# Moving GpSimd's share of the first half of a fused attention and MLP kernel to VectorE, with a scheduler that counts overlapping operations

## The chip, the cores and the metric

The kernel runs on one core of a Trainium2 chip. The metric is the device time of one execution in microseconds (us). Five engines work side by side: PE (TensorE, the matmuls), DVE (VectorE), ACT (ScalarE), POOL (GpSimd) and SP (SyncE, which issues nearly all DMAs). Each executes its own list of instructions strictly in order, and semaphores make one list wait for another.

## The reference, cut to what matters

Attention within chunks of 64 rows, and then an MLP with a hard-swish gate, all in 32-bit floating point:

```python
scores = scale * np.matmul(q_c, k_c.transpose(0, 1, 2, 4, 3))   # chunks of 64 rows, head size 64
scores = scores - np.max(scores, axis=-1, keepdims=True)
attn = np.exp(scores)
attn = attn / (np.sum(attn, axis=-1, keepdims=True) + 1e-09)
out = np.matmul(attn, v_c)            # 8 batches, 8 heads, 576 rows: x is 4608 x 512
h = x @ w_in                          # 512 x 2048
g = h * np.clip(h + 3.0, 0.0, 6.0) / 6.0
return (g @ w_out).astype(np.float32) # 2048 x 512
```

## The kernel before, in words

The 4608 tokens are cut into nine blocks of 512. Block 0 goes through the MLP in the plain way; blocks 1 to 8 go as four pairs (s = 0 to 3), and each pair's two matrix products are done by a scheme with seven block products in place of eight (Winograd's form of Strassen's), which needs sums and differences of the operands. Each product is made in three passes of PE over a high and a low part of both operands (lines 351 to 353), so every operand is split: ACT casts the high part, and another engine subtracts it from the whole, which leaves the low part.

All work is a list of named steps, each with an engine, a cost, the steps it comes after, and what it issues (`work.add`). `Schedule.order` plays the list through once at build time: an engine whose time is free takes, of the steps that are ready, the one that is due first. The order in which steps are taken is the order of the instructions on each engine. The costs are used for nothing else. One rule in it charges a DVE step whose name begins with an entry of `BOTH` extra time while a POOL step is planned beside it (`SHARED`).

The steps that matter here, by their names (u is 0 to 15, p is 0 to 7, k is 0 to 7):

- `lowera{k}`, `lowerb{k}` (L210): the low part of a piece of w_in (a) or w_out (b). `LOWER_ON_POOL` puts b2 to b7 on POOL. Each w_in piece is needed by two tiles `a{j}`, `b{j}` of the first product on PE, each w_out piece by two tiles `c{j}` of the second.
- `whole{u}`, `comb{u}`, `top{u}`, `less{u}s`, `send{u}` (L450, L455, L460, L463, L468): the sums of the weights for the pairs: whole weights (from SBUF on DVE, from DRAM on SP), four subtractions of 128x256, the high part on ACT, the low part, and the store to DRAM on SP. u = 0 to 7 is w_out, 8 to 15 w_in. `LESS_ON_POOL` puts `less0s` to `less7s` on POOL, `COMBS` puts `comb8` to `comb11` there. The tile that `comb` works in, and the one that `top` and `less` write, have two buffers each: `whole{u}` waits for `less{u-2}s`, and `top{u}` for `send{u-2}`.
- `x0.s0` to `x0.s3b` (L570, L574): sums of the first pair's inputs; all but `x0.s0`, `x0.s0c` and `x0.s1` stand on POOL. `x0.5l`, `x0.6l`, `x0.7l`, `x0.4l` (L581) are their low parts.
- `t1.0.p`, `t2.0.p` (L962, L965): sums of the first pair's gates, on POOL. The same sums of the later pairs (L947, L949) are on POOL too, and stay there.
- `gate...` (L377, L761), `u2`, `u4`, `s7`, `s3`, `s4` (L873): DVE's work on each tile that PE finishes. PE's accumulators are few (2 of one kind, 4 of the other), so a late gate stops PE.
- `max`, `sum`, `share` and `turn` with a unit's number: softmax of half a block and its transposes on PE; `turn30` waits for `share30` (L281).
- `f{i}.0.p`: the seven first products of pair 0 (i is the product, p the tile, here 4 to 7). `f5.0.4` is the first that reads sums of weights: `top12`, `less12s`, and `x0.5l`.
- `s0.n`: the second products of pair 0; `ul0.i.k` and `m0.i.k` (L984, L987, L990) make their operands on DVE.

On PE the program runs in this order: softmax of block 0, then the tiles of block 0 and of half of blocks 1 and 2 (to about 172 us), the first products of pair 0 (to 226 us), its second products (to about 313 us), and then pairs 1 to 3, which differ only in where the next pair's attention stands.

Of the kernel before, what the change touches and what calls it, by code (L numbers as in the profile page):

```python
# [31 lines left out]
NFP = NFT // 2  # L32
NPL = 4
# [8 lines left out]
FILL = (2.0, 4.0)  # L42
LAG = 2
ROWS = ["30", "31", "40", "41"]
XDVE = ["x0.s0c"]
SHARED = 0.6
BOTH = ("lower", "join", "whole", "less", "comb", "share", "glow", "ul", "m0", "m1", "m2", "m3", "x0.", "x1.", "x2.", "x3.")
LESS_ON_POOL = list(range(8))
XPOOL = []
ULPOOL = []  # L50
LOWER_ON_POOL = [f"b{i}" for i in range(2, 8)]
APART = 2
EDGE = 32
HASTE = 5.0
# [4 lines left out]
PART = STEP / 4  # L59
SECOND = STEP * (17 + 2 * NPL) + PART * 7 * (NFP - NPL)  # L60
STEPS = SECOND - PART * 7 * (NFP - NPL)
COMBS = [8, 9, 10, 11]


class Schedule:
# [21 lines left out]
    def order(self):  # L87
        then = {n: [] for n in self.steps}
        left = {}
        for n, (_, _, after, _) in self.steps.items():  # L90
            left[n] = len(after)
            for a in after:
                then[a].append(n)
        sorted_, more = [n for n in self.steps if not left[n]], dict(left)
        for n in sorted_:
            for m in then[n]:
                more[m] -= 1
                if not more[m]:
                    sorted_.append(m)
        assert len(sorted_) == len(self.steps)  # L100
        latest = {}
        for n in reversed(sorted_):
            latest[n] = min([self.due[n]] + [latest[m] - self.steps[m][1] - SETTLE for m in then[n]])
        queue = {n: (latest[n] if self.first[n] is None else self.first[n] - 1e6, i) for i, n in enumerate(self.steps)}
        ready = [(0.0, i, n) for i, n in enumerate(self.steps) if not left[n]]
        heapq.heapify(ready)
        waiting, free, at, now = {}, {}, {}, 0.0
        while len(at) < len(self.steps):
            while ready and ready[0][0] <= now:
                _, _, n = heapq.heappop(ready)  # L110
                heapq.heappush(waiting.setdefault(self.steps[n][0], []), (queue[n], n))
            for engine, names in waiting.items():
                if names and free.get(engine, 0.0) <= now:
                    (due, _), n = names[0]
                    end = now + self.steps[n][1]
                    if engine == "DVE" and n.startswith(BOTH):
                        end += SHARED * max(0.0, min(end, free.get("POOL", 0.0)) - now)
                    soon = [t for t, _, m in ready if self.steps[m][0] == engine and 2 * t < now + end and queue[m][0] < due - HASTE]
                    if soon and engine != "SP":
                        free[engine] = min(soon)  # L120
                        continue
                    heapq.heappop(names)
                    at[n], free[engine] = (now, end), end
                    for m in then[n]:
                        left[m] -= 1
                        if not left[m]:
                            t = max(at[a][1] + (0.0 if a[:5] == m[:5] == "fetch" else LAND if self.steps[a][0] == "SP" else 0.0 if self.steps[a][0] == self.steps[m][0] == "PE" else SETTLE)
                                    for a in self.steps[m][2])
                            heapq.heappush(ready, (t, len(at), m))
            now = min([t for t, *_ in ready] + [max(now, free[e]) for e, names in waiting.items() if names], default=now)  # L130
        return sorted(at.items(), key=lambda s: s[1][0])
# [3 lines left out]
def tile_kernel(ctx: ExitStack, tc: tile.TileContext, qk_in, v_in, weights, out):  # L135
# [293 lines left out]
    def in_dram(m, p):  # L429

        return "ab"[m] + str(p // 2) in KEPT
# [405 lines left out]
    for u in [*range(NFP), *range(NFP + NPL, 2 * NFP), *range(NFP, NFP + NPL)]:  # L837
        m, p = 1 - u // NFP, u % NFP
        whole, combine, high, lower, send, send_own = sum_steps(m, p)
        due = STEPS - 8 + 4 * (u - 7) if u < NFP else STEPS - 3 + PART * 7 * (p - NPL) if p >= NPL else SECOND + 10 + 12 * p  # L840
        last = [f"f3.0.{p}"] if u >= NFP + NPL else []
        work.add(f"own{u}", "SP", 2.35, ["lower" + "ab"[m] + str((p + NFP * f) // 2) for f in range(2)], send_own)
        work.add(f"whole{u}", *(("SP", 1.57) if in_dram(m, p) else ("DVE", 1.38)), ["room", *work.take("a", 2, f"whole{u}", [f"less{u}s"])], whole)
        work.add(f"comb{u}", *(("POOL", 4.2, [f"whole{u}"], lambda f=combine: f(POOL)) if u in COMBS else ("DVE", 1.70, [f"whole{u}"], lambda f=combine: f(DVE))))
        work.add(f"top{u}", "ACT", 1.05, [f"comb{u}", *work.take("hl", 2, f"top{u}", [f"send{u}", *last])], high)
        work.add(f"less{u}s", *(("POOL", 2.5, [f"top{u}"], lambda f=lower: f(POOL)) if u in LESS_ON_POOL else ("DVE", 1.22, [f"top{u}"], lambda f=lower: f(DVE))), due=due)
        work.add(f"send{u}", "SP", 3.15, [f"less{u}s"], send, due=due + (4 if u < NFP else 12))
        stored += [f"own{u}", f"send{u}"]
# [104 lines left out]
    def add_units(s):  # L953
        plain = {"gate2.": NFT, "gate4.": NFT + NFP, "gate7.": 2 * NFT + NFP}

        def both(name, pp):
            return [f"gate{plain[name] + 2 * pp + k}" if s == 0 and 2 * pp < NPL and name in plain else f"{name}{s}.{2 * pp + k}" for k in range(2)]

        if s == 0:
            for p in range(NFP):  # L960
                gates = [f"gate{2 * NFT + p}", f"gate{NFT + p}"] if p < NPL else [f"gate3.0.{p}", f"gate2.0.{p}"]
                work.add(f"t1.0.{p}", "POOL", 1.45, gates, lambda p=p: POOL.tensor_tensor(  # L962
                    out=gate_of(0, 1, p), in0=gate_of(0, 1, p), in1=gate_of(0, 0, p), op=ALU.subtract))
                free = {0: [f"out{et}" for et in range(NET)], 1: [f"u2.0.{NFP - 1}"], 2: [f"s7.0.{NFP - 1}"], 3: [f"s3.0.{NFP - 1}", f"s4.0.{NFP - 1}"]}[p // 2]
                work.add(f"t2.0.{p}", "POOL", 1.45, [f"t1.0.{p}", f"gate{2 * NFT + NFP + p}" if p < NPL else f"gate7.0.{p}", *free], lambda p=p: POOL.tensor_tensor(  # L965
                    out=t2_of(p), in0=gate_of(1, 1, p), in1=gate_of(0, 1, p), op=ALU.subtract))
        made_by = {1: "gate2.", 5: "t1.", 6: "t2.", 2: "gate4.", 3: "gate7."}
        for i in ORDER_B:
            for pp in range(NFP // 2):
                high, low = f"uh{s}.{i}.{pp}", f"ul{s}.{i}.{pp}"  # L970
                r, c = WHERE[i]
                src = lambda i=i, pp=pp, r=r, c=c: t2s_of(pp) if i == 6 else gates_of(r, c, pp)
                after = both(made_by[i], pp) if i in made_by else [f"m{s}.{i}.{pp}"]

                slot, before = next_slot(s, high, [f"s{s}.{NFP * ORDER_B.index(i) + 2 * pp + 1}"
                                                   if not (s == NSUP - 1 and i == 3) else f"s{s}.{SLOTS - 4 + pp}"])

                def top(i=i, pp=pp, src=src, slot=slot):
                    g_ops[s, i, pp] = w_tile(f"a{slot}", F32R)
                    ACT.copy(out=g_ops[s, i, pp][:, :, 0], in_=src())  # L980

                work.add(high, "ACT", 1.05, [*after, *before], top)
                on = (s, i, pp) in ULPOOL
                work.add(low, *(("POOL", 2.5) if on else ("DVE", 1.22)), [high], lambda i=i, pp=pp, src=src, on=POOL if on else DVE: on.tensor_tensor(  # L984
                    out=g_ops[s, i, pp][:, :, 1], in0=src(), in1=g_ops[s, i, pp][:, :, 0].bitcast(F32), op=ALU.subtract))
                if i == 5:
                    work.add(f"m{s}.7.{pp}", "DVE", 1.22, [f"ul{s}.1.{pp}", *both("t2.", pp)], lambda pp=pp: DVE.tensor_tensor(  # L987
                        out=gates_of(0, 0, pp), in0=t2s_of(pp), in1=gates_of(0, 0, pp), op=ALU.subtract))
                elif i == 6:
                    work.add(f"m{s}.4.{pp}", "DVE", 1.22, [f"ul{s}.5.{pp}", *both("t2.", pp), *both("gate4.", pp)], lambda pp=pp: DVE.tensor_tensor(  # L990
                        out=gates_of(0, 1, pp), in0=gates_of(1, 0, pp), in1=t2s_of(pp), op=ALU.subtract))
# [135 lines left out]
```

## Time and profile before

| | us |
|---|---|
| median of 3 runs | 799.24 (799.12 to 799.25) |
| the profiled execution | 800.39 |
| its span, first to last instruction | 798.6 |
| PE busy in the span | 778.8 |
| DVE busy in the span | 647.6 |
| POOL busy in the span | 161.2 |

The median lies 1.15 us under the profiled execution, and 1.8 us of that execution lie outside its span. "Busy" counts the time in which an engine had an instruction in execution; an instruction that is held up counts as busy too. A timeline row gives the start, the duration, the engine, the line, the operation, the tiles with their shape and how many instructions are merged, and in brackets how long the engine was idle before it and which instruction ended that.

### The profile page before, as it was taken

To read this page: it belongs to the slowest core of one execution; us is meant where nothing else is said; L and a number is where in the kernel's file an instruction comes from. 1 tells how busy PE (TensorE), PEld (TensorE's weight loads), DVE (VectorE), ACT (ScalarE), POOL (GpSimd) and SP (SyncE) were. 2 spreads that over 40 slices of the span, in tenths; PEclk is the share of its full clock that TensorE was granted. 3 is DMA by queue.
4 is the path that set the end of the run, shared out by engine and by line. 5 is a ranking of instruction groups with operands and counts; after the bars stand their busy time and mean duration, and the time that the engine had idled before them with its cause. 6 is when DMAs were issued, how large, how long until landed. Compare 5 with 4: busy or idle time off the path is not lost.

```text
span 798.6 us, 14046 instructions
## 1 busy us (share of the span) xinstructions
PE 778.8 (98%) x5601; PEld 637.9 (80%) x5603; DVE 647.6 (81%) x758; ACT 396.8 (50%) x593; POOL 161.2 (20%) x105
## 2 busy tenths in 40 slices
PE   8999999978999999999999999999999999999998
PEld 4788878766787888888888888888888888888887
DVE  6898999999899869868898786787998657669851
ACT  3998753356477654334654443335653424355330
POOL 0011242663290120322210001332100013221000
PEclk9999999998999999999999999999999999999999
DMA  9998998864957999666665876576656665566572
GB/s 374 384 412 293 347 324 306 264 219 142 304 190 251 332 313 368 204 195 241 209 241 198 285 268 205 190 241 246 215 195 219 222 207 193 190 197 209 192 232 106
DMA packets 69425, 198.05 MB, mean 248 GB/s; under 512 B 7024, under 2 KB 19568, under 8 KB 65008
## 3 DMA queue, kind: packets, MB, share of 16 engines
q1 hardware_dynamic: 69216, 197.03, 72.0%
q8 instruction: 44, 0.72, 0.4%
q14 instruction: 21, 0.17, 0.1%
q10 hardware_dynamic: 144, 0.13, 0.0%
HBM read 153.09 MB, written 44.04 MB: 247 GB/s over the span
## 4 chain that ended last, share of the span: by engine, by line
PE 80%; DVE 14%; DMA 2%; ACT 2%; issue 1%; POOL 1%; SPq 0%; DVEq 0%; ACTq 0%; POOLq 0%
PE acc L351 18%; PE acc L352 18%; PE acc L353 18%; PE h L352 6%; PE h L351 6%; PE h L353 6%; DVE a L455 4%; PE two L243 2%; PE two L293 2%; PE h L319 2%; DVE wb L761 1%; DVE a L450 1%; DVE e L281 1%; DMA qk<-qk_in 1%; DVE wa L984 1%
## 5 line engine op out<-in xcount | busy, mean ns | idle before, releaser
L351 PE MATMUL acc<-wa,ws 128*128 128x512 f32 (+1 forms) x536 | 209.3, 391 | 0.0
L353 PE MATMUL acc<-wa,ws 128*128 128x512 f32 (+1 forms) x536 | 207.8, 388 | 0.0
L352 PE MATMUL acc<-wa,ws 128*128 128x512 f32 (+1 forms) x536 | 207.8, 388 | 0.0
L980 ACT CAST wa<-wb 128x1024 fp32r<-128x1024 f32 x96 | 100.5, 1053 | 99.4 <-PE acc L353 60.3
L984 DVE TENSOR_TENSOR wa<-wb,wa 128x1024 fp32r<-128x1024 f32 x96 | 126.1, 1322 | 26.4 <-ACT wa L980 26.3
L351 PEld LDWEIGHTS acc<-wa,ws 128*128 128x128 f32 x536 | 100.7, 188 | 20.9 <-issue 0.3
L353 PEld LDWEIGHTS acc<-wa,ws 128*128 128x128 f32 x536 | 100.6, 188 | 20.6
L352 PEld LDWEIGHTS acc<-wa,ws 128*128 128x128 f32 x536 | 100.7, 188 | 20.1
L947 POOL TENSOR_TENSOR wb<-wb 128x512 f32<-128x512 f32 x24 | 32.0, 1332 | 361.0 <-DVE wb L761 361.0
L758 ACT ACTIVATE r<-acc,half 128x512 f32<-128x512 f32 x90 | 61.5, 687 | 41.6 <-DVE acc L873 36.8
L758 ACT ACTIVATE r<-h,half 128x512 f32<-128x512 f32 x38 | 26.2, 689 | 98.6 <-DVE h L873 93.9
L761 DVE SCALAR_TENSOR_TENSOR wb<-r,acc 128x512 f32<-128x512 f32 x90 | 60.8, 681 | 5.6 <-ACT r L758 5.3
L352 PE MATMUL h<-wa,ws 128*128 128x512 f32 (+1 forms) x144 | 55.2, 383 | 0.0
L353 PE MATMUL h<-wa,ws 128*128 128x512 f32 (+1 forms) x144 | 55.2, 383 | 0.0
L351 PE MATMUL h<-wa,ws 128*128 128x512 f32 (+1 forms) x144 | 55.2, 383 | 0.0
L873 DVE TENSOR_TENSOR u<-h,p 128x512 f32<-128x512 f32 x32 | 22.0, 690 | 31.6 <-PE h L353 31.5
L873 DVE TENSOR_TENSOR acc<-acc,u 128x512 f32<-128x512 f32 x48 | 33.2, 697 | 10.3 <-PE acc L353 10.0
L455 DVE TENSOR_TENSOR a<-a 128x256 f32<-128x256 f32 x48 | 40.2, 838 | 1.2
L949 POOL TENSOR_TENSOR g<-wb,wb 128x512 f32<-128x512 f32 x24 | 38.0, 1584 | 1.9
L761 DVE SCALAR_TENSOR_TENSOR wb<-r,h 128x512 f32<-128x512 f32 x38 | 25.9, 683 | 12.6 <-ACT r L758 12.6
L210 POOL TENSOR_TENSOR wb<-u,wb 128x1024 fp32r<-128x1024 f32 x6 | 16.9, 2832 | 88.8 <-ACT wb L207 72.6
L351 PE MATMUL acc<-wa,wa 128*128 128x512 f32 x88 | 34.9, 396 | 0.0
(202 smaller groups left out, 1496.1 us busy)
## 6 DMA issues: line engine op xcount, KB each, us to landing
ws<-b SPq DMA_DIRECT2D x84, 512.0 KB, 4.6
ws<-a SPq DMA_DIRECT2D x72, 512.0 KB, 4.4
qk<-qk_in SPq DMA_DIRECT2D x17, 1024.0 KB, 7.7
wa<-b SPq DMA_DIRECT2D x28, 512.0 KB, 5.7
a<-wa SPq DMA_DIRECT2D x40, 256.0 KB, 5.8
v<-v_in SPq DMA_DIRECT2D x17, 512.0 KB, 5.2
wa<-w_in_out SPq DMA_DIRECT2D x8, 1024.0 KB, 11.2
wb<-w_in_out SPq DMA_DIRECT2D x8, 1024.0 KB, 9.5
```

What stands on the lines that cost most here:

```text
L210: engine.tensor_tensor(out=w[i][:, :, 1], in0=t["a"], in1=w[i][:, :, 0].bitcast(F32), op=ALU.subtract)
L351: PE.matmul(ps, lhsT=a_h, rhs=b_h, start=first, stop=False, skip_group_check=more)
L352: PE.matmul(ps, lhsT=a_h, rhs=b_l, start=False, stop=False, skip_group_check=more)
L353: PE.matmul(ps, lhsT=a_l, rhs=b_h, start=False, stop=last, skip_group_check=more)
L455: engine.tensor_tensor(out=to, in0=x, in1=y, op=op)
L758: ACT.activation(out=t["r"], in_=ps(), func=AF.Relu, bias=half, scale=1.0 / 6.0)
L761: work.add("gate" + name, "DVE", 0.69, ["relu" + name, *more], lambda: DVE.scalar_tensor_tensor(out=out(), in0=t["r"], scalar=1.0, in1=ps( ...
L873: return lambda: DVE.tensor_tensor(out=out(), in0=x(), in1=y(), op=ALU.add)
L947: work.add(id_("t1."), "POOL", 1.45, [id_("gate3."), id_("gate2.")], lambda f=gq: POOL.tensor_tensor(out=f(0, 1), in0=f(0, 1), in1=f(0, 0) ...
L949: work.add(id_("t2."), "POOL", 1.45, [id_("t1."), id_("gate7.")], lambda f=gq, p=p: POOL.tensor_tensor(out=t2_of(p), in0=f(1, 1), in1=f(0, ...
L980: ACT.copy(out=g_ops[s, i, pp][:, :, 0], in_=src())
L984: work.add(low, *(("POOL", 2.5) if on else ("DVE", 1.22)), [high], lambda i=i, pp=pp, src=src, on=POOL if on else DVE: on.tensor_tensor(ou ...
```

## The change

Every table that puts work of the first half on POOL is emptied, and the t1 and t2 steps of pair 0 go to DVE; POOL's first arithmetic instruction is now `t1.1.0`, of the second pair. In `Schedule.order` an engine is counted as free 0.08 us (DVE) or 0.1 us (ACT) before its step ends, and two planned costs of DVE steps are changed (`whole` 1.38 to 1.28, `comb` 1.70 to 1.88). These costs only set the order.

```diff
-XDVE = ["x0.s0c"]
+XDVE = ["x0.s0c", "x0.s2", "x0.s2b", "x0.s3", "x0.s3b"]
 SHARED = 0.6
+OVERLAP = {"DVE": 0.08, "ACT": 0.1}
...
-LESS_ON_POOL = list(range(8))
+LESS_ON_POOL = []
 XPOOL = []
+TPOOL = False
 ULPOOL = []
-LOWER_ON_POOL = [f"b{i}" for i in range(2, 8)]
+LOWER_ON_POOL = []
...
-COMBS = [8, 9, 10, 11]
+COMBS = []
...
-                    at[n], free[engine] = (now, end), end
+                    at[n], free[engine] = (now, end), end - OVERLAP.get(engine, 0.0)
...
-        work.add(f"whole{u}", *(("SP", 1.57) if in_dram(m, p) else ("DVE", 1.38)), ...
+        work.add(f"whole{u}", *(("SP", 1.57) if in_dram(m, p) else ("DVE", 1.28)), ...
-        work.add(f"comb{u}", *(("POOL", 4.2, ...) if u in COMBS else ("DVE", 1.70, ...)))
+        work.add(f"comb{u}", *(("POOL", 4.2, ...) if u in COMBS else ("DVE", 1.88, ...)))
...
-                work.add(f"t1.0.{p}", "POOL", 1.45, gates, lambda p=p: POOL.tensor_tensor(
+                work.add(f"t1.0.{p}", *(("POOL", 1.45) if TPOOL else ("DVE", 0.69)), gates, lambda p=p: (POOL if TPOOL else DVE).tensor_tensor(
...
-                work.add(f"t2.0.{p}", "POOL", 1.45, [f"t1.0.{p}", ...
+                work.add(f"t2.0.{p}", *(("POOL", 1.45) if TPOOL else ("DVE", 0.69)), [f"t1.0.{p}", ...
```

Line numbers after the change are 2 higher. Three places in the order of instructions follow; in them `hl` is the tile of `top` and `less`, `a` the tile of `comb`, `wa`, `wb` and `g` with numbers are buffers of operands and gates.

First, DVE between `comb12` and `share30`, before: `comb12`, `x0.6l`, `less12s`, `gate34`, `x0.7l`, `gate35`, `comb13`, two small steps, `u2.0.4`, `share30`.

```order
L455 TENSOR_TENSOR a<-a 128x256 x4
L581 TENSOR_TENSOR wa_1902<-wb_1406,wa_1902 128x2x512
L463 TENSOR_TENSOR hl<-a,hl 128x4x256
L761 SCALAR_TENSOR_TENSOR wb_1592<-r,h 128x512
L581 TENSOR_TENSOR wa_1949<-wb_1783,wa_1949 128x2x512
L761 SCALAR_TENSOR_TENSOR wb_1592<-r,acc 128x512
L455 TENSOR_TENSOR a<-a 128x256 x4
L277 TENSOR_SCALAR z<-z 128x16
L278 RECIPROCAL z<-z 128x16
L873 TENSOR_TENSOR g_2022<-h,g_1994 128x512
L281 TENSOR_TENSOR e<-e,z 128x1024
```

The same stretch now, from the row after the one that follows `comb12`: `x0.s3`, `gate34`, `x0.6l`, `less12s`, `x0.7l`, `gate35`, `less7s`, `x0.s3b`, two small steps, `gate42`, `share30`.

```order
L576 TENSOR_TENSOR wb_1841<-xc,wb_1412 128x1024
L763 SCALAR_TENSOR_TENSOR wb_1602<-r,h 128x512
L583 TENSOR_TENSOR wa_1908<-wb_1412,wa_1908 128x2x512
L465 TENSOR_TENSOR hl<-a,hl 128x4x256
L583 TENSOR_TENSOR wa_1940<-wb_1841,wa_1940 128x2x512
L763 SCALAR_TENSOR_TENSOR wb_1602<-r,acc 128x512
L465 TENSOR_TENSOR hl<-a,hl 128x4x256
L576 TENSOR_TENSOR wb_1841<-wb_1841,xc 128x1024
L279 TENSOR_SCALAR z<-z 128x16
L280 RECIPROCAL z<-z 128x16
L763 SCALAR_TENSOR_TENSOR wb_1739<-r,h 128x512
L283 TENSOR_TENSOR e<-e,z 128x1024
```

`x0.s3`, `less7s` and `x0.s3b` came in from POOL, `gate41` (not shown, it follows `comb12` now) and `gate42` moved, and `comb13` went behind `share30`.

Second, DVE around `share31` (L281), before: `m0.7.0`, `ul0.5.1`, `ul0.5.2`, `m0.7.1`, two small steps, `share31`, `ul0.5.3`, `ul0.6.0`, `ul0.6.1`.

```order
L987 TENSOR_TENSOR wb_1388<-g_2009,wb_1388 128x2x512
L984 TENSOR_TENSOR wa_2497<-wb_1592,wa_2497 128x2x512
L984 TENSOR_TENSOR wa_2515<-wb_2140,wa_2515 128x2x512
L987 TENSOR_TENSOR wb_1592<-g_2418,wb_1592 128x2x512
L277 TENSOR_SCALAR z<-z 128x16
L278 RECIPROCAL z<-z 128x16
L281 TENSOR_TENSOR e<-e,z 128x1024
L984 TENSOR_TENSOR wa_2546<-wb_1406,wa_2546 128x2x512
L984 TENSOR_TENSOR wa_2551<-g_2009,wa_2551 128x2x512
L984 TENSOR_TENSOR wa_2560<-g_2418,wa_2560 128x2x512
```

Now: `ul0.5.1`, two small steps, `share31`, `ul0.5.2`, `ul0.5.3`, five of the eight t2 steps, `ul0.6.0`, and two more t2 steps.

```order
L986 TENSOR_TENSOR wa_2471<-wb_1602,wa_2471 128x2x512
L279 TENSOR_SCALAR z<-z 128x16
L280 RECIPROCAL z<-z 128x16
L283 TENSOR_TENSOR e<-e,z 128x1024
L986 TENSOR_TENSOR wa_2491<-wb_2078,wa_2491 128x2x512
L986 TENSOR_TENSOR wa_2495<-wb_1412,wa_2495 128x2x512
L967 TENSOR_TENSOR g_2527<-wb_1497,wb_1362 128x512 x2
L967 TENSOR_TENSOR g_2536<-wb_1739,wb_1602 128x512 x2
L967 TENSOR_TENSOR g_2550<-wb_2065,wb_2078 128x512
L986 TENSOR_TENSOR wa_2538<-g_2527,wa_2538 128x2x512
L967 TENSOR_TENSOR g_2550<-wb_2065,wb_2078 128x512
L967 TENSOR_TENSOR g_2571<-wb_1841,wb_1412 128x512
```

Two m steps and `ul0.5.2` went behind `share31`, and the t2 steps stand between `share31` and the next softmax.

Third, PE around `turn11` (L293), before: the last three passes of tile `b11`, `turn11`, the first pass of `c7`.

```order
L351 MATMUL h<-xd,wa_847 128x512
L352 MATMUL h<-xd,wa_847 128x512
L353 MATMUL h<-xd,wa_847 128x512
L293 MATMUL two<-ident,e 128x128 x8
L351 MATMUL acc<-g_836,wb_783 128x512
```

Now: the last three passes of tile `a11`, `turn11`, the first pass of `b11`.

```order
L353 MATMUL h<-xa,wa_833 128x512
L354 MATMUL h<-xa,wa_833 128x512
L355 MATMUL h<-xa,wa_833 128x512
L295 MATMUL two<-ident,e 128x128 x8
L353 MATMUL h<-xd,wa_833 128x512
```

`turn11` stands six passes earlier. PE's order differs in seven more places by one to four steps; among them `turn31` stands ahead of `s0.11` now, six passes earlier too. PE's instructions are the same in number.

## Rows read from the trace of the kernel before

**Rows 1.** The page's busy time, share and instructions of each engine.

```profile
PE 778.8 (98%) x5601; PEld 637.9 (80%) x5603; DVE 647.6 (81%) x758; ACT 396.8 (50%) x593; POOL 161.2 (20%) x105
```

**Rows 2.** Timeline of PE: the instructions before which it was idle longest after 100 us.

```profile
105.64 0.50 PE L351 MATMUL h<-xb,wa 128*128 128x512 f32 x1 [0.28 <-DVE r L377]
...
108.29 1.06 PE L293 MATMUL two<-ident,e 128*128 128x128 f32 x8 [0.99 <-DVE e L281]
...
152.29 0.50 PE L352 MATMUL h<-xd,wa 128*128 128x512 f32 x1 [1.51 <-DVE xd L340]
...
178.77 0.80 PE L351 MATMUL acc<-wa,hl 128*128 128x512 f32 x1 [4.65 <-ACT hl L460]
...
189.63 1.06 PE L293 MATMUL two<-ident,e 128*128 128x128 f32 x8 [2.27 <-DVE e L281]
...
213.22 0.50 PE L351 MATMUL acc<-xd,hl 128*128 128x512 f32 x1 [0.64 <-DVE g L873]
...
243.09 1.06 PE L293 MATMUL two<-ident,e 128*128 128x128 f32 x8 [1.01 <-DVE e L281]
```

**Rows 3.** Windows of 5 us; last three columns: PE's granted clock, DMA share, GB/s.

```profile
180.00:185.00 5.00, 4.97 (x13) 3.94 (x14) 4.93 (x6) 5.00 (x18) 4.35 (x3) 0.56 0.81 267
...
190.00:195.00 5.00, 4.84 (x96) 3.68 (x98) 5.00 (x8) 2.29 (x3) 0.00 (x0) 1.00 0.00 0
```

**Rows 4.** Timeline of PE: passes of one shape that follow each other.

```profile
184.45 0.40 PE L351 MATMUL acc<-wa,hl 128*128 128x512 f32 x1
...
184.92 0.39 PE L353 MATMUL acc<-wa,hl 128*128 128x512 f32 x1
185.15 0.39 PE L351 MATMUL acc<-wa,hl 128*128 128x512 f32 x1
```

**Rows 5.** Groups by line and shape, DVE, 40 to 178 us: busy us, mean ns.

```profile
L455 DVE TENSOR_TENSOR a<-a 128x256 f32<-128x256 f32 x36 | 30.8, 855 | 0.9
...
L384 DVE TENSOR_TENSOR g<-r,g 128x512 fp32r<-128x512 f32 x14 | 13.1, 937 | 0.4 <-ACT g L381 0.4
L450 DVE TENSOR_TENSOR a<-wb 128x512 f32<-128x512 f32 x12 | 9.9, 863 | 0.0
...
L281 DVE TENSOR_TENSOR e<-e,z 128x1024 f32<-128x1024 f32 x4 | 8.1, 2023 | 0.0
```

**Rows 6.** Single lines over the whole span: shortest, median and longest in ns.

```profile
L384 DVE TENSOR_TENSOR g<-r,g x16: 679/684/2477, 31.3 to 120.6; 128x512 fp32r<-128x512 f32 x16
...
L281 DVE TENSOR_TENSOR e<-e,z x17: 1211/1218/3022, 14.0 to 604.8; 128x1024 f32<-128x1024 f32 x17
```

**Rows 7.** Timeline of DVE: two combs, two wholes, and three low parts in a row.

```profile
110.47 1.28 DVE L450 TENSOR_TENSOR a<-wb 128x512 f32<-128x512 f32 x2
...
149.25 1.79 DVE L455 TENSOR_TENSOR a<-a 128x256 f32<-128x256 f32 x4
...
172.09 5.51 DVE L455 TENSOR_TENSOR a<-a 128x256 f32<-128x256 f32 x4
...
244.00 3.49 DVE L984 TENSOR_TENSOR wa<-g,wa 128x1024 fp32r<-128x1024 f32 x3
```

**Rows 8.** Groups of POOL, 40 to 300 us; idle time before each and its ends.

```profile
L463 POOL TENSOR_TENSOR hl<-a,hl 128x1024 fp32r<-128x1024 f32 x8 | 20.7, 2585 | 36.5 <-ACT hl L460 23.0 <-DMA qk<-qk_in 9.5 <-DMA b<-hl 4.1
```

**Rows 9.** A window of 20 us: busy PE, PEld, DVE, ACT, POOL, clock, DMA.

```profile
60.00:80.00 20.00, 20.00 (x211) 16.36 (x210) 16.74 (x22) 17.45 (x21) 3.10 (x1) 1.00 0.85 293
```

**Rows 10.** Timelines of DVE and PE: `share11`, `turn11`, `share31`, `share40`, `turn40`.

```profile
77.73 1.22 DVE L281 TENSOR_TENSOR e<-e,z 128x1024 f32<-128x1024 f32 x1
...
79.87 0.81 PE L293 MATMUL two<-ident,e 128*128 128x128 f32 x6
...
241.72 1.23 DVE L281 TENSOR_TENSOR e<-e,z 128x1024 f32<-128x1024 f32 x1
...
263.42 1.22 DVE L281 TENSOR_TENSOR e<-e,z 128x1024 f32<-128x1024 f32 x1
...
267.38 1.03 PE L293 MATMUL two<-ident,e 128*128 128x128 f32 x8
```

More of the change, by code (lines that the diff above doesn't have):

```diff
@@ L842, in tile_kernel @@
         work.add(f"own{u}", "SP", 2.35, ["lower" + "ab"[m] + str((p + NFP * f) // 2) for f in range(2)], send_own)
-        work.add(f"whole{u}", *(("SP", 1.57) if in_dram(m, p) else ("DVE", 1.38)), ["room", *work.take("a", 2, f"whole{u}", [f"less{u}s"])], whole)
-        work.add(f"comb{u}", *(("POOL", 4.2, [f"whole{u}"], lambda f=combine: f(POOL)) if u in COMBS else ("DVE", 1.70, [f"whole{u}"], lambda f=combine: f(DVE))))
+        work.add(f"whole{u}", *(("SP", 1.57) if in_dram(m, p) else ("DVE", 1.28)), ["room", *work.take("a", 2, f"whole{u}", [f"less{u}s"])], whole)
+        work.add(f"comb{u}", *(("POOL", 4.2, [f"whole{u}"], lambda f=combine: f(POOL)) if u in COMBS else ("DVE", 1.88, [f"whole{u}"], lambda f=combine: f(DVE))))
         work.add(f"top{u}", "ACT", 1.05, [f"comb{u}", *work.take("hl", 2, f"top{u}", [f"send{u}", *last])], high)
@@ L961, in add_units @@
                 gates = [f"gate{2 * NFT + p}", f"gate{NFT + p}"] if p < NPL else [f"gate3.0.{p}", f"gate2.0.{p}"]
-                work.add(f"t1.0.{p}", "POOL", 1.45, gates, lambda p=p: POOL.tensor_tensor(
+                work.add(f"t1.0.{p}", *(("POOL", 1.45) if TPOOL else ("DVE", 0.69)), gates, lambda p=p: (POOL if TPOOL else DVE).tensor_tensor(
                     out=gate_of(0, 1, p), in0=gate_of(0, 1, p), in1=gate_of(0, 0, p), op=ALU.subtract))
                 free = {0: [f"out{et}" for et in range(NET)], 1: [f"u2.0.{NFP - 1}"], 2: [f"s7.0.{NFP - 1}"], 3: [f"s3.0.{NFP - 1}", f"s4.0.{NFP - 1}"]}[p // 2]
-                work.add(f"t2.0.{p}", "POOL", 1.45, [f"t1.0.{p}", f"gate{2 * NFT + NFP + p}" if p < NPL else f"gate7.0.{p}", *free], lambda p=p: POOL.tensor_tensor(
+                work.add(f"t2.0.{p}", *(("POOL", 1.45) if TPOOL else ("DVE", 0.69)), [f"t1.0.{p}", f"gate{2 * NFT + NFP + p}" if p < NPL else f"gate7.0.{p}", *free], lambda p=p: (POOL if TPOOL else DVE).tensor_tensor(
                     out=t2_of(p), in0=gate_of(1, 1, p), in1=gate_of(0, 1, p), op=ALU.subtract))
```

## The prediction, made before the changed kernel was run

> **What bounds the kernel now.** I read the busy times first: PE is busy for 778.8 of 798.6 us, DVE for 647.6, POOL for 161.2 [rows 1]. So only what PE loses can be won, some 20 us, and from the first busy times alone one would say that DVE has room. The second view is the timeline of PE, read for the idle time before an instruction. After 100 us I take the seven that other engines' lateness makes, and the reader is to see that they lie between 105 and 245 us and that six of the seven name DVE: 0.28 and 0.99 at 105.6 and 108.3, 1.51 at 152.3, 4.65 at 178.8, 2.27 at 189.6, 0.64 at 213.2 and 1.01 at 243.1, 11.35 us together [rows 2]. The longest names ACT (`top12`), but ACT's step had itself waited for `comb12` on DVE, which ends at 172.09 + 5.51 = 177.60 [rows 7], about the length of that ACT step before PE goes on.
>
> After that wait PE is slow as well: in 180 to 185 its granted clock is 0.56 of full speed, near the lower of its two levels (1.2 against 2.4 GHz), while after the wait of 2.27 us the clock of 190 to 195 is 1.00 [rows 3]. The twelve passes of `f5.0.4` and `f6.0.4` take from 178.77 [rows 2] to 184.45; passes of this shape otherwise start 0.23 apart (184.92, 185.15) [rows 4]. That is 5.68 in place of 12 x 0.23 = 2.76: 2.9 us. In all 14.25 us of PE's time are lost after 100 us to DVE being late.
>
> Third view: DVE by groups from 40 to 178 us, against the same lines elsewhere. There DVE hardly rests, but part of its time is not work. The 36 instructions of L455 are nine combs and take 30.8 us [rows 5]; a comb alone takes 1.79 and `comb12` took 5.51 [rows 7]: 30.8 - 9 x 1.79 = 14.7 too much. L384: 13.1 - 14 x 0.684 = 3.5. L450: 9.9 - 6 x 1.28 = 2.2. L281: 8.1 - 4 x 1.218 = 3.2 [rows 5 to 7]. Together 23.6 us, all in instructions that read two SBUF tiles while POOL works.
>
> **The change part by part.** In the first half POOL becomes empty, and I count those 23.6 us as returned by 178 us. What DVE gets is priced by pitch, not by duration: three low parts of 128x1024 take 3.49, so each adds 1.14 behind the first [rows 7]; a 128x512 subtraction adds 0.60, the second of the pair of 1.28 [rows 7]; a comb 1.79.
>
> *Up to `comb12`.* DVE has 6 `lowerb`, 7 `less` and 2 `x0` steps more ahead of it, and `gate41` less: 15 x 1.14 - 0.60 = 16.5. So `comb12` ends at 177.6 + 16.5 - 23.6 = 170.5, or at 167.2 if DVE also fills the 3.26 us that it was idle in 60 to 80 (20 - 16.74) [rows 9]. Then `gate41`, `x0.s3`, `gate34`, `x0.6l`, `less12s` follow: 2 x 0.60 + 3 x 1.14 = 4.6, so `less12s` is done at 171.8 to 175.1. Without its stalls PE would be at `f5.0.4` at 178.77 - 4.65 - 0.28 - 0.99 - 1.51 = 171.3; with the delay of 2.0 that follows, at 173.3, and its third pass, which reads the low part, 0.5 later. `share30` has `x0.7l`, `gate35`, `less7s`, `x0.s3b`, two small steps and `gate42` before it: about 10.8 after `comb12`, 178.0 to 181.3, against PE's 173.3 + 24 x 0.23 = 178.8. `comb13`, which stood ahead of it, is now behind. So of 4.65 + 2.9 + 2.27 between 0 and 2.5 remains; I take 0.8, nearer the low end, since much of DVE's idle time can be filled. The 1.51 at 152.3 goes: `rest21` has 12 steps more ahead, less than what is returned by then, and 0.28 and 0.99 go with them (`share20`: six `lowerb` more, `gate14` less, 6.2, against L384's 3.5, part of L281's 3.2 and the idle time). What is late next there is `gate14`, which went behind `share20`; it has no slack, and I count nothing for it.
>
> *Before 100 us.* `turn11` now stands six passes earlier, 6 x 0.23 = 1.4, and `share11` has two `lowerb`, a `lowera`, a join and a `glow` more ahead: 4 x 1.14 + 0.60 = 5.2. `share11` ended at 77.73 + 1.22 = 78.95, 0.92 before `turn11` [rows 10]. With nothing filled or returned PE waits 5.2 + 1.4 - 0.9 = 5.7; with DVE's idle 3.26 us filled [rows 9], 2.4; and it is 0 if L384's surplus of 3.5 is returned before it as well. A gain is excluded, since PE has no wait there now. I take 2.0, near the middle value, because DVE's idle time is where the added steps stand and a little of L384's surplus lies ahead of it (its longest instruction took 2.48 in place of 0.68 [rows 6], somewhere between 31 and 121 us).
>
> *190 to 300 us.* Here the change adds 16 t steps and 4 combs: 16 x 0.60 + 4 x 1.79 = 16.8. `u4.0.5` has `comb15` ahead of it now: 0 to 1.8, as no wait stands at `f3.0.5` now; I take 0.4, the lower part, since the gates that DVE makes just before it are not needed at once. Between `share31` and `share40` DVE took (263.42 + 1.22) - (241.72 + 1.23) = 21.7, and now (eight t2 steps and two combs more, three steps of 1024 in and five out) 8 x 0.60 + 2 x 1.79 - 2 x 1.14 = 6.1 more, 27.8. PE took 267.38 - 243.09 = 24.3 from `turn31` to `turn40`, and takes 1.4 more with `s0.11` in between: 25.7 [rows 2, 10]. The 2.1 that are short must come from `share31` being early: it stands about 4.5 us behind the last gate, `gate4.0.7` (three t1 steps, two of 1024, two small ones), and PE has eleven steps of six passes, 15 us, from there to `turn31`. So 0 to 2.1; I take 0.6. The waits of 0.64 and 1.01 go by the same lead.
>
> *Order and costs.* The planner's new numbers cost nothing by themselves; what they move is in the counts above. In the pairs 1 to 3 some neighbours on DVE change places; PE hides that, as it never waits there.
>
> Sum: 14.25 - 2.0 - 0.8 - 0.4 - 0.6 = 10.45. Against the profiled execution, 800.39 (span 798.6 and 1.8 outside it), that gives 789.9; the median of the runs lies 1.15 lower: 788.8.
>
> **The rivals.** (A) The wait moves. DVE is nearly full from 40 to 178 us; if the early, middle and late costs come out at their upper ends, 5.7 + 2.5 + 1.8 + 2.1 = 12.1, only 2.15 is left: 800.39 - 2.15 - 1.15 = 797.1. Half way between, with costs of 8.0: 793.0. For it: ACT is also busy for 17.45 of 20 us in 60 to 80 [rows 9], so DVE may not find its steps ready. Against it: the costs have different causes, and a delay of PE in one place shortens the next.
>
> (B) Slower: DVE inherits the waits of POOL. POOL sat idle for 36.5 us before its eight `less` steps, 13.6 of them put down to DMA [rows 8]: `top{u}` waits for `send{u-2}`, and `less{u}s` for `top{u}`. On POOL that held up little; in DVE's list everything behind it waits, gates and softmax too. It decides as soon as a store takes longer than DVE needs from one `less` to the next but one. If the 13.6 come whole, `comb12` ends at 167.2 + 13.6 = 180.8, 3.2 later than before, the four later waits stay, and with the early 2.0, less the 1.27 won at 105 to 108, the run takes 800.39 + 3.2 + 2.0 - 1.3 = 804.3, less 1.15: 803.2. Against it: the stores start earlier when `less` is done earlier, and DVE has `comb` and gates between.
>
> (C) The change doesn't do what it says: DVE's surplus is not POOL's doing, and it stays in part. If 10 of the 23.6 us stay, `comb12` ends at 177 to 180, the waits at `f5.0.4` and `turn30` stay with the slow clock (9.8 of the 14.25), and the costs of 3.8 take most of the rest: 800.39 - 0.6 - 1.15 = 798.6. For it: nothing in the rows; the long combs stand beside POOL's work.
>
> (D) Slower by far: DVE is saturated, nothing returns, and the added work counts in full. Then `comb12` comes 16.5 - 3.3 = 13.2 later, and the run takes 800.39 + 13.2 - 1.15 = 812.4. Against it: the comb of 5.51 beside one of 1.79 [rows 7]. The Trainium skill ("Perfetto Trace Analysis", Optimizing Scalar/DVE Operations) says that work of a saturated VectorE may be worth moving to GpSimd, which is what this change undoes, and adds that the two share a read port of SBUF, so that it might not help. The first half of that rule would give D's time, the second the forecast's; the combs in the trace bear out the second.
>
> **How the numbers follow.** The forecast, 785 to 793, has 0.52; A, at 793 to 797.6, has 0.23; A's far end and C, within 0.2%, 0.09; B has 0.13 and D 0.03. Less than 0.2% (1.6 us, 797.6 to 800.8) can hardly be told from no change. So faster 0.75, same 0.09, slower 0.16. The range from 784.5 (all costs zero: 800.39 - 14.25 - 1.15 = 785.0) to 800 leaves out some 0.03 below and 0.16 above.
>
> **What would show it.** In the changed profile: combs all near 1.79; no wait of 4 us before `f5.0.4` and no granted clock near 0.56 after it; a wait of some 2 us before `turn11`; `turn30` and `turn40` with waits under 1.5; DVE's busy time within a few us of 647.6, and no POOL work before the second pair. It is wrong if PE waits longer than 4 us for DVE anywhere, if DVE's idle time names ACT's `top` (L460 before the change) or DMA for more than 5 us, or if combs of 3 us and more remain.

## The result and the profile after the change

| | before | after |
|---|---|---|
| median of 4 runs, us | 799.25 (799.12 to 800.19) | 785.85 (785.42 to 786.71) |
| profiled execution, us: its time, its span | 800.39, 798.6 | 786.71, 784.9 |
| predicted median, us | | 788.8 (784.5 to 800.0) |

The ratio is 0.9831, with a 95% interval of 0.9814 to 0.9848: 13.4 us faster, where 10.45 was forecast.

The page's busy line of the changed kernel answers to [rows 1].

```profile
PE 774.1 (99%) x5603; PEld 636.1 (81%) x5603; DVE 647.4 (82%) x808; ACT 397.3 (51%) x593; POOL 69.6 (9%) x55
```

TensorE's time outside its matmuls fell from 798.6 - 778.8 = 19.8 us to 784.9 - 774.1 = 10.8. The same matmuls also took 4.7 us less. 2.9 of it is the slow stretch of the clock behind `f5.0.4`, which is gone; 1.6 lies ahead of the first tile, where the granted clock was 0.89 before and is 1.00 now, which is not the change's doing (see the last section); some 2 are passes around the waits that are gone; and a new slow stretch behind 298 us takes 1.9 back. The 9.0 and the 4.7 make the 13.7 us of the span. VectorE does 50 instructions more in the same busy time, 647.4 for 647.6: what it took over is what it no longer loses.

The timeline of PE after the change (start, us, shape, count, and in brackets the idle time and its end) at the places of [rows 2, 10]. The first row and the last are the only waits of over a microsecond behind the start-up, at 29.61 and 298.13; between them stand `turn11`, `f5.0.4`, `turn30` and `turn40`.

```profile
29.61 0.50 PE L353 MATMUL h<-xa,wa 128*128 128x512 f32 x1 [1.24 <-DVE r L379]
...
78.17 1.04 PE L295 MATMUL two<-ident,e 128*128 128x128 f32 x8
...
170.02 0.39 PE L353 MATMUL acc<-wa,hl 128*128 128x512 f32 x1
...
175.47 1.03 PE L295 MATMUL two<-ident,e 128*128 128x128 f32 x8
...
250.18 1.03 PE L295 MATMUL two<-ident,e 128*128 128x128 f32 x8
...
298.13 0.47 PE L353 MATMUL acc<-wa,ws 128*128 128x512 f32 x1 [2.07 <-DMA ws<-a]
```

All seven waits of [rows 2] are gone; 4.65 before `f5.0.4` has become nothing. The windows of the changed kernel (busy PE, PEld, DVE, ACT, POOL, then PE's granted clock, DMA share, GB/s) show the clock there, to be read against [rows 3], and behind the new wait at 298.

```profile
171.00:176.00 5.00, 5.00 (x26) 4.17 (x25) 4.90 (x9) 0.75 (x1) 0.00 (x0) 1.00 1.05 344
...
298.00:303.00 5.00, 4.87 (x14) 3.87 (x15) 4.93 (x8) 3.66 (x5) 0.00 (x0) 0.66 0.92 306
```

The groups of DVE from 40 to 178 us (busy us, mean ns of one, idle before) answer to [rows 5]: four lines that took 855, 937, 863 and 2023 ns on average are down to what one takes alone.

```profile
L457 DVE TENSOR_TENSOR a<-a 128x256 f32<-128x256 f32 x40 | 16.8, 423 | 1.0
...
L386 DVE TENSOR_TENSOR g<-r,g 128x512 fp32r<-128x512 f32 x13 | 8.8, 679 | 0.2 <-ACT g L383 0.2
...
L452 DVE TENSOR_TENSOR a<-wb 128x512 f32<-128x512 f32 x12 | 7.6, 682 | 0.0
...
L283 DVE TENSOR_TENSOR e<-e,z 128x1024 f32<-128x1024 f32 x5 | 6.1, 1213 | 0.0
```

The timeline of DVE after the change at `comb12` (159.87), `less12s` (165.04) and `share30` (171.10). The comb of 5.51 us [rows 7] takes 1.79.

```profile
159.87 1.79 DVE L457 TENSOR_TENSOR a<-a 128x256 f32<-128x256 f32 x4
...
165.04 1.22 DVE L465 TENSOR_TENSOR hl<-a,hl 128x1024 fp32r<-128x1024 f32 x1
...
171.10 1.21 DVE L283 TENSOR_TENSOR e<-e,z 128x1024 f32<-128x1024 f32 x1
```

### The profile page after: what moved, and what is told of

Read it like the earlier page. It is cut to its first block, busy times and chain, and to the rows that moved or that the text cites. A ratio compares the mean times of both kernels' runs of the same rounds, so it can differ in the third digit from the quotient of the medians.

```text
span 784.9 us, 14014 instructions
## 1 busy us (share of the span) xinstructions
PE 774.1 (99%) x5603; PEld 636.1 (81%) x5603; DVE 647.4 (82%) x808; ACT 397.3 (51%) x593; POOL 69.6 (9%) x55
## 4 chain that ended last, share of the span: by engine, by line
PE 93%; DMA 3%; DVE 2%; ACT 1%; issue 0%; SPq 0%; DVEq 0%; ACTq 0%
PE acc L353 21%; PE acc L355 21%; PE acc L354 21%; PE h L353 8%; PE h L355 8%; PE h L354 8%; PE two L245 2%; PE two L295 2%; DMA wa<-b 2%; PE h L321 1%; DMA ws<-a 1%; PE h L171 1%; DMA out_t<-o 1%; PE two L321 1%; DVE o L1007 0%
## 5 line engine op out<-in xcount | busy, mean ns | idle before, releaser
L353 PEld LDWEIGHTS acc<-wa,ws 128*128 128x128 f32 x536 | 100.9, 188 | 23.6 <-issue 2.5
L353 PE MATMUL acc<-wa,wa 128*128 128x512 f32 x88 | 34.8, 396 | 0.0
L355 PE MATMUL acc<-wa,wa 128*128 128x512 f32 x88 | 34.3, 390 | 0.0
L354 PE MATMUL acc<-wa,wa 128*128 128x512 f32 x88 | 34.3, 390 | 0.0
## 6 DMA issues: line engine op xcount, KB each, us to landing
wa<-w_in_out SPq DMA_DIRECT2D x8, 1024.0 KB, 12.4
```

The costliest lines, as they stand in the source:

```text
L353: PE.matmul(ps, lhsT=a_h, rhs=b_h, start=first, stop=False, skip_group_check=more)
L354: PE.matmul(ps, lhsT=a_h, rhs=b_l, start=False, stop=False, skip_group_check=more)
L355: PE.matmul(ps, lhsT=a_l, rhs=b_h, start=False, stop=last, skip_group_check=more)
```

## The experiments

The "surplus" of a stretch is the sum, over its VectorE instructions, of the duration less a base: the duration that the shortest fifth of the same line and shape does not exceed in the same trace. From 0 to 300 us it was 38 us before the change and 0.7 after. Medians, with the ratio to the kernel before run beside them (799.0 to 799.5 in these runs):

| run | us | ratio, 95% | surplus to 300 us |
|---|---|---|---|
| extra subtractions on GpSimd | 810.66 | 1.0145 (1.0126 to 1.0165) | 21.6 |
| extra constant writes | 786.90 | 0.9848 (0.9832 to 0.9864) | 1.3 |
| extra one-input multiplications | 797.43 | 0.9973 (0.9959 to 0.9988) | 15.2 |
| change without the accounting | 807.05 | 1.0097 (1.0075 to 1.0118) | 0.4 |
| accounting without the move | 802.99 | 1.0052 (1.0032 to 1.0073) | 42.7 |
| old order, steps on VectorE | 794.66 | 0.9937 (0.9916 to 0.9958) | 0.8 |
| new order, steps on GpSimd | 803.00 | 1.0041 (1.0026 to 1.0057) | 42.4 |
| half the accounting | 792.64 | 0.9910 (0.9886 to 0.9935) | 0.7 |
| half as much again on VectorE | 790.88 | 0.9890 (0.9866 to 0.9914) | 0.6 |
| two waits taken off | 787.10 | 0.9844 (0.9819 to 0.9870) | 0.6 |
| ... and later pairs on VectorE | 787.88 | 0.9850 (0.9822 to 0.9877) | 0.4 |

The theories by their names in the expectations: "contention", that GpSimd's work on SBUF lengthens VectorE's, and that taking it away returns the time whatever the order; "hand-over", that GpSimd took 2.4 us and began late on chains that others wait for; "order", that the accounting for overlap brought the steps forward. Two came up on the way: "plan in step", that a fixed order is good where the planner's times for VectorE agree with the chip's, and "chance", that every order has its own luck.

### Does GpSimd hold VectorE up, and what kind of its work does?

Three kernels keep the changed one's order and give GpSimd work on a tile of its own, released behind the matmuls at which it had worked before.

```
+            twins = [POOL.tensor_tensor(out=spare_t, in0=spare_t, in1=spare_t, op=ALU.subtract) for _ in range(...)]
+            if k == 0: tc.add_manual_dep(twins[0].ins, latest_mm[0].ins.name, SYNC, reason="twin")
second:      POOL.memset(spare_t, 0.0)
third:       POOL.tensor_scalar(out=spare_t, in0=spare_t, scalar1=1.0, scalar2=None, op0=ALU.mult)
```

> The changed kernel, with GpSimd given 128x256 subtractions of a tile of its own, at the 40-odd places of the matmul order where it had worked before, about 75 us in sum; nobody waits for them and nothing reads them. 'Contention': most of the loss comes back, 792 to 800; surplus of VectorE below 300 us 20 to 40 us, combines of 2.5 us and more, a wait of over 2 us before f5.0.4. 'Hand-over': 785 to 787, since no chain goes through GpSimd. 'Order': 785 to 787.

> The same places and about the same time of GpSimd work, but writes of a constant, which read nothing. If any work of GpSimd on SBUF holds VectorE up: as with the subtractions, 792 to 800 and 20 to 40 us of surplus. If only work with inputs in SBUF does: 785 to 787 and under 3 us of surplus. 'Hand-over' and 'order': 785 to 787.

> The extra work of GpSimd once more, now multiplications of its own 128x256 tile by a constant: one input in SBUF instead of two or none. If one input is enough to hold VectorE up, 10 us and more of surplus below 300 us and 792 to 810, as with subtractions; if it takes two, under 3 us of surplus and 785 to 788, as with the constant writes.

The combs of the three (shortest, median and longest in ns; in the kernel before the longest took 2623), subtractions first, then writes, then multiplications:

```profile
L469 DVE TENSOR_TENSOR a<-a x64: 410/426/830, 110.9 to 303.9; 128x256 f32<-128x256 f32 x64
```

```profile
L469 DVE TENSOR_TENSOR a<-a x64: 414/425/428, 106.8 to 279.7; 128x256 f32<-128x256 f32 x64
```

```profile
L469 DVE TENSOR_TENSOR a<-a x64: 409/426/615, 107.3 to 290.0; 128x256 f32<-128x256 f32 x64
```

Nobody waits for this extra work. Its amount differs: 118 subtractions keep GpSimd busy for 117 us, 222 constant writes for 70 and 170 multiplications for 196. The writes have no effect on the combs and none on the time that is clear of the noise. The subtractions cost 24.8 us against the changed kernel, more than the forecast 792 to 800; of the wait of over 2 us that was expected at `f5.0.4` came 0.60, but other waits are longer. I read the excess as VectorE having both the moved steps and the surplus, which no run parts. So GpSimd's being slow or late on the path ("hand-over") isn't needed for the loss; its reading of SBUF is. The multiplications say that one input is enough: 15.2 us of surplus and 797.43, within what was given for that case. The surplus comes back, and with it TensorE's wait for VectorE before a gate or a share. One such wait in the first kernel is 4.62 us long:

```profile
273.43 1.94 PE L305 MATMUL two<-ident,e 128*128 128x128 f32 x8 [4.62 <-DVE e L293]
```

### Is it the order?

```
first:   -OVERLAP = {"DVE": 0.08, "ACT": 0.1}      +OVERLAP = {}
second:  XDVE, LESS_ON_POOL, TPOOL, LOWER_ON_POOL and COMBS as before; OVERLAP and the two new costs stay
```

> The changed kernel with the new order's accounting undone (OVERLAP empty), all of GpSimd's steps still on VectorE. Theory 'contention' (GpSimd's two-input subtractions hold VectorE's up, so removing them returns VectorE's 38 us of surplus whatever the order): 785 to 788, no seven old waits, VectorE surplus below 300 us under 2 us. Rival 'order' (the overlap subtracted from an engine's free time is what brought the steps forward): 794 to 799, waits of over 1 us back at the turns and before f5.0.4. Rival 'hand-over' (GpSimd takes 2.4 us and starts late where VectorE takes 1.22, so the chains through it end late): as contention, 785 to 788. The start-up, 1.4 us shorter after the change, should go back to 22.98 us if it came from the accounting.

> GpSimd gets all its old steps back (subtractions less and lower, combines 8 to 11, t1 and t2, the first pair's operands); the accounting and the two new costs stay. 'Contention': 796 to 800, surplus of VectorE below 300 us 33 to 40 us, some combines at 3 us and over. 'Order': 785 to 789. 'Hand-over': 796 to 800, as contention. The share of the accounting alone is what this gains on the kernel before; I expect 0 to 1.5 us, from the start-up.

Neither half of the change helps when the planner makes a new order for it alone. The first is the surprise: no surplus, and yet slower than before, by 8.1 us. "Contention" as I had put it was refuted as the whole cause. The second has more surplus (42.7 us) and takes longer than I gave it (33 to 40, 796 to 800): the accounting without the move costs time. The wait before the first product's fetched weights is back, with the clock at half behind it (timeline of PE, then windows, without the accounting):

```profile
173.18 0.79 PE L353 MATMUL acc<-wa,hl 128*128 128x512 f32 x1 [4.70 <-ACT hl L462]
```

```profile
173.00:178.00 5.00, 4.31 (x9) 2.98 (x10) 4.97 (x7) 1.89 (x7) 0.00 (x0) 0.50 0.48 165
```

VectorE's waits from 40 to 178 us (us in sum, times, longest) tell why `less12s` ended at 174.85 there and at 166.26 in the changed kernel. Without the accounting:

```profile
DVE wa L212 <- ACT wa L209: 1.7, 1, 1.7
DVE g L403 <- PE acc L355: 1.7, 2, 1.4
DVE wb L763 <- ACT r L760: 1.3, 1, 1.3
DVE a L452 <- DMA wb<-u: 1.3, 1, 1.3
...
DVE g L386 <- ACT g L383: 0.8, 1, 0.8
```

The changed kernel, the longest two of its waits:

```profile
DVE wb L763 <- ACT r L760: 0.8, 1, 0.8
DVE wb L572 <- ACT xa L338: 0.6, 1, 0.6
```

An engine takes its instructions in the listed order. Without the accounting the list has steps whose inputs the chip hasn't made yet when VectorE comes to them: 9.8 us of such waits from 40 us to `less12s`, against 2.3. These 7.5 us are most of the 8.6 by which `less12s` is late. That they come of the planner holding VectorE for slower than it is, is not shown: there the chip was 3.3 us ahead of its plan, but with half the accounting (below) it was behind, and VectorE sat idle nearly as long.

To part the two, two kernels keep an order and change only the engine that runs the early steps:

```
first, in the kernel before:   lower, less, comb, x0.s2 to x0.s3b, t1.0, t2.0:   f(POOL) -> f(DVE), planned as before
second, in the changed kernel: the same steps                                    f(DVE) -> f(POOL), planned as changed
```

> The kernel before with its order of issue kept instruction for instruction on TensorE, and only the engine of GpSimd's early steps changed: VectorE runs them at the same places of the order. It parts the change of engine from the new order. New theory 'plan in step' (a fixed order is good when the plan's times for VectorE agree with the chip's; the chip ran 13.1 us behind the plan at the first subtraction that the first product fetches in the kernel before, 0.0 after the change, 17.2 with the accounting alone, and 3.3 ahead with the engines alone): the 38 us of surplus go and some 40 us of work come, so the chip should be within 3 us of the old plan (166.8 us there) and the time 785 to 791. 'Order' (it takes the new order to gain): 797 or more. 'Placement replanned is bad in itself', as the 807 of the run without the accounting might say: 800 and more.

> The other half: the changed kernel's order kept, GpSimd runs again what it ran before. 'Contention' and 'plan in step': surplus of VectorE below 300 us 30 to 42 us, the chip 10 to 20 us behind the plan at that subtraction, 797 to 808. 'Order': under 790.

| | steps on GpSimd | steps on VectorE |
|---|---|---|
| old order | 799.5 | 794.7 |
| new order | 803.0 | 785.9 |

In the old order the move is worth 4.8 us, with `less12s` 5.1 behind the old plan; both lie outside what I gave for "plan in step" (785 to 791, within 3 us). In the new one it is worth 17.1. The new order costs 3.5 us where GpSimd still holds VectorE up, and gains 8.8 where it doesn't. In the old order `turn30` still waits for its share, as [rows 2] had it:

```profile
181.11 1.94 PE L293 MATMUL two<-ident,e 128*128 128x128 f32 x8 [2.65 <-DVE e L281]
```

### How much accounting?

```
first:   OVERLAP = {"DVE": 0.04, "ACT": 0.05}
second:  OVERLAP = {"DVE": 0.12, "ACT": 0.1}
```

> The changed kernel with half the accounting (VectorE 0.04, ScalarE 0.05); its plan has that subtraction end at 171.7 us instead of 166.3. 'Plan in step': the chip is ahead of the plan and VectorE sits idle in its order for things that come later, 3 to 6 us more of it than after the change between 40 and 300 us; 789 to 799, between the full accounting (786) and none (807). Rival 'chance' (any order is as good, the list scheduler only happened on bad ones): 784 to 790 or over 800, with no relation to the drift.

> The changed kernel with too much accounting on VectorE (0.12 for 0.08; ScalarE as it is); the plan has that subtraction end at 163.0 us. 'Plan in step': VectorE is asked for more than it can do, the chip falls 2 to 5 us behind the plan, and TensorE waits for gates and shares of VectorE: 788 to 795. 'Chance': no relation, 784 to 787 as likely as more.

The planner's own time for the end of `less12s`, what the chip made of it, and VectorE's idle time (140 less its busy time from 40 to 180 us):

| accounting on VectorE | planned end | measured end | idle, 40 to 180 | time |
|---|---|---|---|---|
| 0 | 178.2 | 174.9 | 12.4 | 807.1 |
| 0.04 | 171.7 | 173.9 | 10.8 | 792.6 |
| 0.08 | 166.3 | 166.3 | 4.0 | 785.9 |
| 0.12 | 163.0 | 165.9 | 5.1 | 790.9 |
| old order and engines | 166.8 | 180.0 | 6.6 | 799.5 |
| old engines, 0.08 | 163.9 | 181.1 | 7.2 | 803.0 |

The window behind the best of these (busy DVE, clock, DMA share, GB/s), and behind the run without the accounting:

```profile
40.00:180.00 140.00, 135.99 (x190) 1.00 0.91 318
```

```profile
40.00:180.00 140.00, 127.64 (x177) 0.98 0.89 304
```

The best time is where plan and chip agree. But with half the accounting the chip was 2.2 us behind its plan there, not ahead of it as I had expected, so the sign of the gap is no guide. The idle time that the order leaves on VectorE is the better one below 0.08: with half the accounting 6.8 us more than in the changed kernel (as much from 40 to 300, for which I had expected 3 to 6). Above it idle time hardly rises, and TensorE waits instead (1.57 us for a gate at 123.67, 3.45 for a fetch at 302.03). Four points do not show that this curve is smooth: the list scheduler makes another order at each. Both times lie within what "plan in step" gave (789 to 799, 788 to 795), and the first lies outside what "chance" gave (784 to 790 or over 800), but the sign that it rested on is wrong for half the accounting, so why these orders differ stays open beyond VectorE's idle time and TensorE's waits.

### Can the rest be had?

```
+LATE = {"v50": ["fetch31"], "qk60": ["fetch33"]}     (added to what these loads wait for)
 join: [f"shift{i}", f"down{i}"]  ->  [..., "gate0" if i == "b0" else None]
second kernel: also t1 and t2 of the later pairs  POOL.tensor_tensor -> DVE.tensor_tensor
```

> The changed kernel with its two new waits of TensorE attacked by the order alone: the join of the second matrix's first weights waits for the first gate (it stood ahead of it on VectorE and cost the third tile 1.24 us at 29.6), and the loads of V for block 5 and of Q and K for block 6 wait until the first fetches of the second pair are issued (they stood ahead of them in SyncE's queue; the fetch landed 2.07 us late at 298.1). 'Plan in step': both waits go, or most of them, and nothing else moves: 782 to 785. Rival 'chance': every new order has a new wait of its own somewhere, 785 to 792.

> As the run before, and the two subtractions t1 and t2 of every pass of the later pairs on VectorE too, so that GpSimd has next to nothing left. 'Contention': VectorE's surplus of 12.2 us after 300 us goes under 2 us, against 48 x 0.69 = 33 us less 0 more work; TensorE hardly waits there, so 781 to 786, within 1.5 of the run before. 'VectorE becomes the bound in the later pairs': over 788.

Neither beats the changed kernel, and the first lies where "chance" had it (785 to 792), not "plan in step" (782 to 785). The wait for the fetch is gone, and the two behind it come out, together as long as it was (timeline of PE, first kernel):

```profile
29.38 0.50 PE L354 MATMUL h<-xa,wa 128*128 128x512 f32 x1 [1.04 <-DVE r L380]
...
177.87 0.50 PE L354 MATMUL acc<-xd,hl 128*128 128x512 f32 x1 [1.64 <-DVE g L876]
...
300.89 0.47 PE L354 MATMUL h<-wa,ws 128*128 128x512 f32 x1 [0.70 <-ACT p L934]
...
306.58 0.50 PE L354 MATMUL acc<-wa,ws 128*128 128x512 f32 x1 [1.36 <-DVE u L876]
```

At 29 the gate still comes late with the join out of its way: 1.04 us for 1.24. `lowera1` still stands ahead of it on VectorE, and waits 1.08 us there for ScalarE. In the second kernel VectorE's surplus after 300 us falls from 12.1 to 1.3 us, as contention has it, and the time does not move (787.88, outside the 781 to 786 and the over 788 that I gave): behind 310 us TensorE waits nowhere for more than 0.25 us in either kernel.

## Why the prediction was right, and where it was not

- **The 14.25 us of waits and slow clock.** Right, all of it went. From just before `turn20` to the end of the first pair (the last pass starts at 313.38 before, at 295.68 after) TensorE's lead on the kernel before grew from 0.34 to 17.70 us, 3.1 more than the 14.25. The seven rows were not all: 1.1 us are four shorter waits that the prediction left out, of 0.04 and 0.15 at 180.0 and 192.5 and two that are longer than the shortest of its seven (timeline of PE before):

```profile
249.18 0.46 PE L243 MATMUL two<-qk 64*64 64x64 f32 x16 [0.45 <-issue]
...
295.13 1.16 PE L319 MATMUL h<-e,v 64*64 64x64 f32 x64 [0.43 <-ACT e L297]
```

  The other 2 us are the steps around each wait, which cost more than the wait itself. Before the change the step into the wait of 0.28 at 105.64 took 0.67 us and the step behind it 0.34, against 0.23 for undisturbed ones.
- **The 23.6 us of surplus returned by `comb12`.** Right in kind, too small. It ended at 161.66, forecast 167.2 to 170.5; `less12s` at 166.26, forecast 171.8 to 175.1. The added work was counted well: the 15 steps more and `gate41` less are just those in the measured order. But the sum was made from four lines, and all lines together lost 28 us from 40 to 180, and VectorE was already 1.9 us ahead at 30 us (`gate0`, `lowera1` and `joinb0`, in whichever order, were done at 29.56, before at 31.42), with a start-up that was 1.4 us shorter in this execution.
- **The costs of 2.0, 0.8, 0.4 and 0.6.** Wrong by being costs at all: no wait stands before `turn11`, `turn30`, `u4.0.5`'s reader or `turn40`. `share11` ended at 78.00, 0.17 before `turn11`: the lowest of the three cases given, but not by its reason. Of L384's surplus only 1.1 us lay ahead of `share11` (one instruction of 1781 ns at 50.2). VectorE filled 3.0 us of idle time (3.5 before, 0.5 after, from 30 us to the end of `share11`), 1.2 us of surplus came back, and at 30 us it was 1.9 us ahead where TensorE, by its wait at 29.61, was ahead by 0.3 at most. So part of the 2.0 was paid at 29.61.
- **What was not forecast.** The wait of 1.24 us at 29.61: `joinb0` and `lowera1` now stand ahead of `gate0` on VectorE. TensorE's lead falls there from 1.43, the shorter start-up, to 0.13; with the same order on both engines and a start-up as long as before (the new order with steps on GpSimd) the wait is there too, 1.22 us. And the wait of 2.07 at 298.13 with the slow clock behind it (0.66), which takes the lead from 17.70 to 13.8, 3.9 us in all: the first fetch of the second pair stands in SyncE's queue behind two loads and two stores, and TensorE, 17 us earlier, now gets there first. These 5.2 us stand in place of the 3.8 of costs. That 785.85 lies so near the forecast 788.8 is in part luck: the gain that was missed, the costs that did not come, the waits that nobody listed and a start-up that varies come near to cancelling.
- **"The planner's new numbers cost nothing by themselves."** This step fell. The instruction counts were taken from the new order and so held its effect, but the text gave the whole gain to VectorE's surplus. The runs give the move alone 4.8 us and the new order 8.8 on top of it, and the move replanned without the accounting loses 8. The new order with the steps on GpSimd loses 3.5.
- **The rivals.** B, VectorE inheriting GpSimd's waits for stores, did not come: before 178 us none of VectorE's waits names a DMA, and from there to 300 us two of 2.3 us do, for loads of its own inputs and a store. C is excluded by the combs. D, that nothing returns, is excluded by VectorE's busy time: it is near full, at 136 of 140 us, but does 50 instructions more in the same 647 us, so the added work is paid from the surplus. The Trainium skill ("SBUF — State Buffer", SBUF: two separate sides) says that a VectorE instruction with two inputs in SBUF and a GpSimd instruction that reads SBUF exclude each other on a shared pair of ports. The subtractions against the constant writes bear that out, 21.6 us against 1.3; the multiplications, with one input, come between (15.2), and there no hold lasted nearly as long as GpSimd's instruction (last section).
- **How sure it could be.** The range held, and the chance of 0.75 for faster was on the right side. That the same engines in another order take 21 us longer stood in no row of the trace before. The prediction was protected from it by counting steps in the order that was to run.

## What to carry to other kernels

Where VectorE is nearly full, look at how its two-input instructions lengthen beside GpSimd's before moving work either way: a subtraction taken back to VectorE may cost it nothing. An order written out ahead is part of the change: here the same engines took 785.9 to 807.1 us by what the planner counted, and the wrong order gave back more than the move gained. Of the four amounts of accounting the best was the one at which the planner's time for one step met the chip's, but the sign of the gap did not foretell the others. Test such a change as a square, each half alone and both: here either half alone, replanned, was slower than the start, while the same move in the old order gained 4.8 us.

## What the runs showed of the hardware

- How long one hold lasts goes with what GpSimd runs. Beside multiplications (one input, 0.85 us for the shortest) a subtraction of a comb took at most 0.615 us, 0.19 more than alone. Beside subtractions (two inputs, 0.61 us for the shortest) it took up to 0.830, 0.40 more, and in the kernel before, where GpSimd's subtractions of 128x1024 take 2.4 us and more, up to 2.623, 2.2 more. So the longest hold seen is a quarter of the one-input instruction, and two thirds or more of the two-input ones. Each of the three longest (2.50 to 2.62 us) ends 0.28 us after the GpSimd instruction beside it does.
- Small one-input instructions of VectorE are held too, and one of them by a constant write. The four of 128x16 that add 1e-9 to the softmax's sums take 160 to 175 ns in the kernel before. Shortest, median and longest with the extra subtractions, the writes and the multiplications, in that order:

```profile
L289 DVE TENSOR_SCALAR z<-z x4: 578/580/612, 181.4 to 295.4; 128x16 f32<-128x16 f32 x4
```

```profile
L289 DVE TENSOR_SCALAR z<-z x4: 164/167/323, 171.8 to 272.1; 128x16 f32<-128x16 f32 x4
```

```profile
L289 DVE TENSOR_SCALAR z<-z x4: 359/362/362, 175.1 to 283.0; 128x16 f32<-128x16 f32 x4
```

- The gates, which read one operand from PSUM, were not lengthened: of the 90 that read `acc` (L775), 35 of them beside GpSimd's work, the kernel with the extra subtractions shows 670 ns for the shortest and 690 for the longest.
- The start-up varies by 1.3 to 1.6 us at the same order. The first matmul of the first tile began at 23.11 with the constant writes and at 21.77 with the multiplications, though these kernels differ only from 47 us on; the granted clock from 8 to 23 us was 0.89 in the first, 1.00 in the second. Before and after the change it was 22.98 at 0.89 and 21.55 at 1.00, and with the changed kernel's order and the steps on GpSimd 23.14 at 0.89; without the accounting it was 20.99 at 1.00. So the 1.4 us there are not the change's. The two rows are the writes' and the multiplications':

```profile
23.11 0.50 PE L381 MATMUL h<-xa,wa 128*128 128x512 f32 x1 [0.25 <-ACT wa L219]
```

```profile
21.77 0.50 PE L381 MATMUL h<-xa,wa 128*128 128x512 f32 x1 [0.25 <-ACT wa L219]
```
